# One sum and one reciprocal of a head's softmax sums in place of two

## The chip, the core and the metric

The kernel runs on one core of a Trainium2 chip. The metric is the device time in microseconds; the median of three runs of the kernel before is 1118.94 us (1118.8 to 1119.47).

The engines are named as in the profile: PE multiplies matrices (PEld are its weight loads), DVE is the vector engine, ACT computes the exponentials and many copies, POOL is GpSimd, SP issues the DMAs. Each engine works through its own queue strictly in the order in which the program was written; semaphores hold an instruction back until what it reads has been written.

## What is computed

Attention with a block-causal mask for 64 heads (batch 8, 8 heads, 576 positions, 64 channels), then a mixer: a low-rank product over the positions and a feed-forward pair of layers over the channels.

```python
scores = scale * np.matmul(q, k.transpose(0, 1, 3, 2))
...
scores = np.where(mask, scores, -1000000000.0)
scores = scores - np.max(scores, axis=-1, keepdims=True)
attn = np.exp(scores)
attn = attn / (np.sum(attn, axis=-1, keepdims=True) + 1e-09)
return np.matmul(attn, v).astype(np.float32)
...
h = xt @ U @ V
u = x + h.transpose(0, 2, 1)
ch = np.maximum(u @ w_ch1, 0.0) @ w_ch2
return (u + ch).astype(np.float32)
```

## The kernel before

**Tiles of a head.** The 576 query rows of a head are cut into five tiles: tile 0 has 64 rows and 64 keys, tiles 1 to 4 have 128 rows and 192, 320, 448 and 576 keys, since the mask lets a row see only the keys up to its block.

**The way of a head.** `softmax` is called three times per head: for tiles 4, 1 and 0 together, for tile 3, and for tile 2. Each call puts the score products on PE (L1233 for the first 14 heads, L1237 and L1238 for the rest), the row maxima on DVE (L1251, into mx), and the exponentials on ACT (L1262, into the tiles p). An exponential also writes the sum of its row into column 0 of ss; column 1 holds the constant 1e-9. `normalise` then adds the two columns (L1278, DVE), takes the reciprocal (L1279, DVE, into rv), and scales each tile p by it on POOL (L1289). Then `transpose` turns the tiles on PE (L1326), copies the result out of its bank on ACT (L1300, ph) and takes the remainder on DVE (L1343, pl), and `apply_v` multiplies with v (L1367 for the first 14 heads, L1383 for the rest). After two heads `mix` does the low-rank product for them (L1409 to L1456).

Before the change `normalise` is called twice per head: once for tiles 4 and 3, as soon as their exponentials are through, and once for tiles 2, 1 and 0. The tiles p, the sums ss, the maxima mx and the reciprocals rv have two buffers each, one for even and one for odd heads.

**The filler.** The feed-forward layers are in two parts. The first (hidden channels 0 to 767, `ffn_chunk`, products on L663 and L688) is given to the planner with a low priority on PE and runs between attention's products once its weights are ready. The second (`block_products`, L912) starts when attention is over and fills the rest of the time.

**What sets the order.** No loop of the source is the order on the engines. Every piece of work is handed to a planner with `add(engine, ns, prio, fn, reads, writes)`: an assumed duration, a priority and the buffers that it reads and writes. `issue` then plays this plan through in assumed time: an engine that is free takes, of the work whose inputs are ready and whose buffers are free, that with the lowest priority number, and writes its instructions into its queue. The order so found is fixed in the program. Each assumed duration is first shifted by up to 2% in a pseudo-random way that depends on the piece's number and on the constant `VARIANT` (L61), so that another `VARIANT`, or one piece more or less, gives other orders everywhere:

```python
ns *= 1 + 0.04 * ((n * 40503 + 7919 * VARIANT) % 65536 / 65536 - 0.5)
```

[...]

Of the kernel before, what the change touches and what calls it, by code (L numbers as in the profile page):

```python
# [57 lines left out]
TAIL = {"PE": 165, "DVE": 78, "ACT": 105, "POOL": 20, "SP": 0}  # L58
INTO = {"PE": 355, "DVE": 60, "ACT": 60, "POOL": 200, "SP": 60}
NEAR, DL, PORT = 130, 3000, 200  # L60
VARIANT = 96  # L61
START = {"DVE": 5750, "ACT": 2750, "POOL": 3300, "SP": 700}
COL = 0.4555
LA, MP = 900.0, 500.0
# [83 lines left out]
class Plan:  # L148
# [8 lines left out]
    def add(self, engine, ns, prio, fn, reads=(), writes=(), hold=(), after=0, port=False):  # L157

        n = len(self.tasks)
        ns *= 1 + 0.04 * ((n * 40503 + 7919 * VARIANT) % 65536 / 65536 - 0.5)  # L160
        deps = set()
        for b in reads:
            deps.update(b.writers)
            b.readers.append(n)
        for b in hold:
            deps.update(b.readers, b.writers)
        for b in writes:
            deps.update(b.readers, b.writers)
            b.writers, b.readers = [n], []
        deps.discard(n)  # L170
        slots = {b for b in (*reads, *writes) if b.pool is not None}
        for b in slots:
            b.users += 1
        self.tasks.append((engine, ns, prio, fn, deps, after, slots, port or engine == "POOL"))
# [105 lines left out]
def attention_then_mixer(  # L280
# [19 lines left out]
    add = plan.add  # L300
# [94 lines left out]
    inverse = [[Buf(iv_t[:, n, x : x + 1]) for x in range(1 + B)] for n in range(3)]  # L395
# [87 lines left out]
    def first_w1(w, bufs, prio, o, gate=()):  # L483
        at = lambda k: (slice(None), k, slice(o * C1, (o + 1) * C1))
        weights_of(
            {"gate": gate, "out": bufs["w1"][o]}, lambda k: w()["w1h"][at(k)], lambda k: w()["w1l"][at(k)],
            [w1[k * P : (k + 1) * P, 2 * o * C1 : 2 * (o + 1) * C1] for k in range(KC)], scales[o], prio, None, C1,
        )
# [34 lines left out]
    def first_w2(w, bufs, prio, o, gate=()):  # L523
        at = lambda k: (slice(None), o * FH + k, slice(None))
        weights_of(
            {"gate": gate, "out": bufs["w2"][o * FH : (o + 1) * FH]}, lambda k: w()["w2h"][at(k)], lambda k: w()["w2l"][at(k)],
            [w2[(o * FH + k) * P : (o * FH + k + 1) * P, :] for k in range(FH)], scales[2 + o], prio, agree if o else None,
        )
        multiply(inverse[o][B], scales[o], scales[2 + o], 2.0 ** -9, prio(FH - 1))
# [655 lines left out]
    def split_v(h, pr):  # L1185
        s = h % 2
        raw, vs = vr_r[h // 2 % 2], vs_r[s]
        mine = raw[:, 5 * s : 5 * s + 5, :]
        if s == 0:
            add(  # L1190
                "SP", 910, pr,
                lambda: nc.sync.dma_start(out=raw[:, 0:10, :], in_=v[h // 2].rearrange("p s j d -> p (s j) d")),
                writes=[raw], after=DL,
            )
        if h < FP:
            return
        hi, lo = vs[:, :, 0:64], vs[:, :, 64:P]
        add(
            "ACT", _act(320, True), pr, lambda: nc.scalar.copy(hi, mine),
            [raw], [vs],  # L1200
        )
        add("POOL", 845, pr, lambda: nc.gpsimd.tensor_sub(lo, mine, f32(hi)), [raw, vs], [vs])
# [69 lines left out]
    def normalise(h, tiles, pr):  # L1272
        ss, rv = ss_r[h % 2], rv_r[h % 2]
        cs = slice(min(tiles), max(tiles) + 1)

        def inverse():

            nc.vector.tensor_reduce(out=rv[:, cs], in_=ss[:, cs, :], op=ALU.add, axis=AX.X)  # L1278
            nc.vector.reciprocal(rv[:, cs], rv[:, cs])  # L1279

        add("DVE", 274, pr, inverse, [ss.parts[i] for i in tiles], [rv.parts[i] for i in tiles])
        for i in tiles:
            rows, w = P if i else 64, P * i + 64
            pt = pt_r[i][h % PB[i]]
            x = pt[:rows, :w]
            to = pt_r[1][h % PB[1]]
            add(
                "POOL", 255 + 0.85 * w, pr,
                lambda x=x, rows=rows, i=i, to=to: nc.gpsimd.tensor_scalar(  # L1289
                    out=x if i else to[:rows, P : P + 64], in0=x, scalar1=rv[:rows, i : i + 1], scalar2=1.0, op0=ALU.mult,  # L1290
                    op1=ALU.mult,
                ),
                [rv.parts[i], pt], [pt if i else to],
            )
# [188 lines left out]
    for h in range(NH):  # L1483
        pr = 1000.0 * h
        if h + 1 < NH:
            split_qk(h + 1, max(pr - LA, 1.0))
        for g, tiles in ((1, (4, 3)), (0, (2, 1, 0))):
            for x in ((4, 1, 0), (3,)) if g else ((2,),):
                softmax(h, x, pr + 10)
            normalise(h, tiles, pr + 10)  # L1490
        for g in (1, 0):
            for part in range(2):
                transpose(h, g, part, pr + 20 + 10 * (1 - g))
            apply_v(h, g, pr + 30)
        if h + 1 < NH:
            split_v(h + 1, pr + 1000)
        if h % 2 == 1:
            mix(h // 2, pr + 40)
        if h == min(WH, NH - 1):
            gate = Buf()  # L1500
            gate.writers = [len(plan.tasks) - 1]
            first_w2(lambda: wa, wab, lambda n: WPB + WP1 * n, 0, [gate])
            first_w1(lambda: wa, wab, lambda n: WP2 + WP3 * n, 1, [gate])
            first_w2(lambda: wa, wab, lambda n: WP4 + WP3 * n, 1, [gate])
# [48 lines left out]
```

## Time and profile before

| | us |
|---|---|
| median of 3 runs | 1118.94 |
| the profiled execution, its time | 1121.03 |
| its span (first to last instruction) | 1119.2 |
| PE, matmuls busy in the span | 1098.7 |
| DVE busy | 986.2 |
| ACT busy | 814.8 |
| POOL busy | 497.5 |

The granted clock of PE is 1.0 in the profiled execution. Matmul ends are modelled, and matmuls overlap, so that a start-to-start distance says more than one matmul's duration. The chain of work that ended last is mostly PE, with ACT's exponentials and DVE behind it:

```profile
PE 63%; ACT 15%; DVE 13%; DMA 4%; issue 3%; POOL 2%; SPq 0%; ACTq 0%; POOLq 0%; DVEq 0%
```

Of the lines that the change touches, POOL's scaling is the costliest group of the whole page by one line (its columns: busy us, mean ns of one, then POOL's idle time just before them and what ended it):

```profile
L1289 POOL TENSOR_SCALAR p<-p,rv 128x448 f32<-128x448 f32 (+4 forms) x320 | 170.3, 543 | 110.3 <-DVE rv L1279 25.5
```

### The profile page before, as it was taken

How to read it: one execution, taken by the hardware profiler on the slowest of the kernel's cores; microseconds unless marked ns; L12 is line 12 of the kernel's file. 1: busy time of each engine (PE TensorE's matmuls, PEld its weight loads, DVE VectorE, ACT ScalarE, POOL GpSimd, SP SyncE). 2: the span in 40 equal slices, each digit the busy share in tenths (PEclk: the TensorE clock that was granted, in tenths of full speed). 3: DMA queues.
4: the chain of work that ended last, by engine and by line, in shares of the span. 5: the costliest groups of instructions: out<-in, count | busy, mean ns of one | idle time of the engine just before them, and what ended most of it. 6: DMA issues, size and time to landing. Idle time of an engine off the chain costs nothing.

```text
span 1119.2 us, 25191 instructions
## 1 busy us (share of the span) xinstructions
PE 1098.7 (98%) x8846; PEld 915.3 (82%) x8846; DVE 986.2 (88%) x2241; ACT 814.8 (73%) x1994; POOL 497.5 (44%) x688
## 2 busy tenths in 40 slices
PE   9999999999999999999999999999999999999998
PEld 7877788888888888888888877777777777777776
DVE  5898898999898998998989767599989999998998
ACT  7887999998989999998988955255555445454543
POOL 5434468887878868778777774100000000000000
PEclk9999999999999999999999999999999999999999
DMA  4544567455454546464452152113223040403111
GB/s 127 160 121 123 155 179 190 132 158 153 118 158 137 151 129 167 115 198 131 137 142 80 40 151 66 44 34 95 75 54 103 27 117 12 128 19 110 34 52 44
DMA packets 76718, 122.11 MB, mean 109 GB/s; under 512 B 9008, under 2 KB 53040, under 8 KB 76592
## 3 DMA queue, kind: packets, MB, share of 16 engines
q1 hardware_dynamic: 76592, 120.51, 37.9%
q8 instruction: 70, 1.15, 0.4%
q14 instruction: 56, 0.46, 0.1%
HBM read 76.23 MB, written 29.49 MB: 94 GB/s over the span
## 4 chain that ended last, share of the span: by engine, by line
PE 63%; ACT 15%; DVE 13%; DMA 4%; issue 3%; POOL 2%; SPq 0%; ACTq 0%; POOLq 0%; DVEq 0%
PE bb L912 37%; ACT p L1262 6%; PE bf L663 6%; PE bf L688 5%; PE ba L1326 4%; DVE pl L1343 3%; DVE mx L1251 3%; PE ba L1383 2%; PE ba L1367 2%; ACT ph L1300 2%; DMA raw<-in_qk_dram 2%; PE bw L1233 1%; ACT tmp L1389 1%; ACT q L1173 1%; POOL p L1289 1%
## 5 line engine op out<-in xcount | busy, mean ns | idle before, releaser
L1289 POOL TENSOR_SCALAR p<-p,rv 128x448 f32<-128x448 f32 (+4 forms) x320 | 170.3, 543 | 110.3 <-DVE rv L1279 25.5
L912 PE MATMUL bb<-ph,w2h 128*128 128x288 f16 x560 | 151.0, 286 | 0.0
L912 PE MATMUL bb<-ph,w2l 128*128 128x288 f16 x560 | 151.0, 286 | 0.0
L912 PE MATMUL bb<-ph,w1h 128*128 128x288 f16 x560 | 148.7, 286 | 0.0
L912 PE MATMUL bb<-ph,w1l 128*128 128x288 f16 x560 | 148.7, 286 | 0.0
L834 ACT CAST ph<-hb 128x576 f16<-128x576 f32 x144 | 84.3, 590 | 83.5 <-PE bb L912 77.8
L912 PEld LDWEIGHTS <-w1h 128*128 128x128 f16 x1120 | 109.6, 98 | 27.5
L912 PEld LDWEIGHTS <-w2h 128*128 128x128 f16 x1120 | 109.6, 98 | 27.5
L912 PE MATMUL bb<-pl,w2h 128*128 128x288 f16 x560 | 123.6, 286 | 0.0
L1343 DVE TENSOR_TENSOR pl<-ba,ph 128x512 fp32r<-128x512 f32 x200 | 106.5, 550 | 10.1 <-ACT ph L1300 7.5
L912 PE MATMUL bb<-pl,w1h 128*128 128x288 f16 x560 | 114.5, 286 | 0.0
L688 PE MATMUL bf<-hh,w2h 128*128 128x288 f16 x384 | 110.3, 287 | 0.1
L688 PE MATMUL bf<-hl,w2h 128*128 128x288 f16 x384 | 109.8, 286 | 0.0
L688 PE MATMUL bf<-hh,w2l 128*128 128x288 f16 x384 | 109.8, 286 | 0.0
L1326 PE MATMUL ba<-ident,p 128*128 128x128 f32 x704 | 106.8, 274 | 2.4 <-POOL p L1289 1.1
L1262 ACT ACTIVATE p<-bw,mx 128x576 f32<-128x576 f32 (+2 forms) x192 | 93.0, 490 | 10.3 <-DVE mx L1251 8.7
L1300 ACT CAST ph<-ba 128x512 fp32r<-128x512 f32 x200 | 94.0, 493 | 3.1 <-PE ba L1326 1.3
L836 DVE TENSOR_TENSOR pl<-hb,ph 128x576 f16<-128x576 f32 x144 | 91.3, 651 | 1.2 <-ACT ph L834 0.4
L688 PEld LDWEIGHTS <-w2h 128*128 128x128 f16 x768 | 75.3, 98 | 20.4 <-issue 1.7
L663 PEld LDWEIGHTS <-w1h 128*128 128x128 f16 x768 | 73.4, 98 | 21.0 <-issue 3.9
L1383 PE MATMUL ba<-ph,vs 128*128 128x256 f32 (+3 forms) x400 | 86.4, 271 | 0.6 <-ACT p L1262 0.5
L1326 PEld LDWEIGHTS ba<-ident,p 128*128 128x128 f32 x704 | 82.2, 141 | 5.3 <-POOL p L1289 2.2
(185 smaller groups left out, 3091.9 us busy)
## 6 DMA issues: line engine op xcount, KB each, us to landing
raw<-in_qk_dram SPq DMA_DIRECT2D x63, 288.0 KB, 3.9
o_d<-ot SPq DMA_DIRECT2D x72, 144.0 KB, 2.0
vr<-in_v_dram SPq DMA_DIRECT2D x32, 320.0 KB, 3.6
ur<-u_d SPq DMA_DIRECT2D x64, 144.0 KB, 2.7
wr<-o_d SPq DMA_DIRECT2D x32, 288.0 KB, 3.0
out_dram<-wr SPq DMA_DIRECT2D x31, 288.0 KB, 2.3
st<-in_w_dram SPq DMA_DIRECT2D x16, 512.0 KB, 4.0
u_d<-ut SPq DMA_DIRECT2D x28, 288.0 KB, 2.1
```

The source lines that it names most:

```text
L663: nc.tensor.matmul(ps[:, :T], w()[wn][:, k, fs], m[k].ap, start=(i == 0), stop=(i == len(ops) - 1))
L688: nc.tensor.matmul(ps[:, :T], w()[wn][:, f, ms], hs[f][x].ap, start=(i == 0), stop=(i == len(ops) - 1))
L834: add("ACT", _act(n * T, True), E, lambda: nc.scalar.copy(h.ap[:, :n, :], x[0]()), [x[1]], [h])
L836: "DVE", _dve(n * T), E, lambda: nc.vector.tensor_sub(l.ap[:, :n, :], x[0](), h.ap[:, :n, :]), [x[1], h], [l],
L912: nc.tensor.matmul(bank[:, i, :T], x()[:, w(k)], p.ap[:, k, :], start=first and n == 0, stop=last and n == len(ops) - 1)
L1251: lambda i=i, at=at: nc.vector.tensor_reduce(out=mx[: P if i else 64, i : i + 1], in_=view(i, at), op=ALU.max, axis=AX.XY if i == 4 else AX.X,
L1262: nc.scalar.activation(out.rearrange("p (j k) -> p j k", j=2) if i == 4 else out, view(i, at), AF.Exp, bias=mx[:rows, i : i + 1], accum_ou ...
L1289: lambda x=x, rows=rows, i=i, to=to: nc.gpsimd.tensor_scalar(out=x if i else to[:rows, P : P + 64], in0=x, scalar1=rv[:rows, i : i + 1], s ...
L1300: add("ACT", _act(n), pr, lambda: nc.scalar.copy(out(), inp()), reads, writes)
L1326: nc.tensor.transpose(out=to, in_=pt_r[i][h % PB[i]][:, j * P : (j + 1) * P], identity=perm.ap)
L1343: "DVE", _dve(m), pr, lambda: nc.vector.tensor_sub(pl[:, low], bank[:, :m], f32(ph[:, low])), [bank, bh], [bl]
L1383: nc.tensor.matmul(bank[0 : c.stop, a:n], vs[:, j, c], x[:, _at(g, j)], start=(i == 0), stop=(i == len(ops) - 1))
```

## The change

`normalise` is called once per head, after all three calls of `softmax`, for the five tiles together: one sum over five columns of ss and one reciprocal over five columns of rv, which depend on all five exponentials. The five scalings on POOL stay five instructions. The assumed duration of the pair is 300 ns in place of 274, and `VARIANT` is 191 in place of 96.

```diff
-VARIANT = 96
+VARIANT = 191
...
-        add("DVE", 274, pr, inverse, [ss.parts[i] for i in tiles], [rv.parts[i] for i in tiles])
+        add("DVE", 300, pr, inverse, [ss.parts[i] for i in tiles], [rv.parts[i] for i in tiles])
...
         for g, tiles in ((1, (4, 3)), (0, (2, 1, 0))):
             for x in ((4, 1, 0), (3,)) if g else ((2,),):
                 softmax(h, x, pr + 10)
-            normalise(h, tiles, pr + 10)
+        normalise(h, (4, 3, 2, 1, 0), pr + 10)
```

Since the planner is run anew, the queues of all engines differ from the first heads on. Three places follow.

DVE, in the middle of attention, the same head in both programs (rv are its reciprocals, ss its sums; mx are maxima of the next heads, pl and xl remainders, hl and ot the filler's). Before:

```order
L1456 TENSOR_REDUCE um_109<-ut_202 128x1
L1278 TENSOR_REDUCE rv_187<-ss_162 128x2
L1279 RECIPROCAL rv_187<-rv_187 128x2
L1415 TENSOR_TENSOR xl_198<-ba_96,xh_197 128x512
L1251 TENSOR_REDUCE mx_185<-ba_98 128x1
L1251 TENSOR_REDUCE mx_186<-bw 128x1 x2
L1251 TENSOR_REDUCE mx_186<-bw 64x1
L671 SCALAR_TENSOR_TENSOR hl<-bf_91,hh 128x288
L1415 TENSOR_TENSOR xh_197<-ba_97,xh_197 64x128
L1278 TENSOR_REDUCE rv_187<-ss_162 128x3
L1279 RECIPROCAL rv_187<-rv_187 128x3
```

Of the change, from the same L1456 on:

```order
L1456 TENSOR_REDUCE um_109<-ut_202 128x1
L361 SCALAR_TENSOR_TENSOR z_102<-st_100,z_102 128x320
L1278 TENSOR_REDUCE rv_187<-ss_162 128x5
L1279 RECIPROCAL rv_187<-rv_187 128x5
L1343 TENSOR_TENSOR pl_192<-ba_97,ph_190 128x512
L1343 TENSOR_TENSOR pl_192<-ba_98,ph_190 128x448
L1343 TENSOR_TENSOR pl_191<-ba_95,ph_189 128x64
```

In place of two pairs with seven rows between them there is one pair, with remainders of other heads behind it.

POOL, some nine heads later, again the same head in both (p_1_173 down to p_1_165 are the head's tiles 4 to 0; q and k are inputs of later heads, t belongs to `mix`). Before:

```order
L1289 TENSOR_SCALAR p_1_173<-p_1_173,rv_188 128x576
L1289 TENSOR_SCALAR p_1_171<-p_1_171,rv_188 128x448
L1179 TENSOR_TENSOR q_1_176<-raw_161,q_1_155 64x576
L1289 TENSOR_SCALAR p_1_169<-p_1_169,rv_188 128x320
L1430 TENSOR_TENSOR t_0_199<-tz_200,t_0_199 32x128
L1289 TENSOR_SCALAR p_1_167<-p_1_167,rv_188 128x192
L1180 TENSOR_TENSOR k_1_158<-raw_161,k_1_179 64x576
L1289 TENSOR_SCALAR p_1_167<-p_1_165,rv_188 64x64
```

Of the change:

```order
L1289 TENSOR_SCALAR p_1_173<-p_1_173,rv_188 128x576
L1289 TENSOR_SCALAR p_1_171<-p_1_171,rv_188 128x448
L1289 TENSOR_SCALAR p_1_169<-p_1_169,rv_188 128x320
L1289 TENSOR_SCALAR p_1_167<-p_1_167,rv_188 128x192
L1289 TENSOR_SCALAR p_1_167<-p_1_165,rv_188 64x64
L1179 TENSOR_TENSOR q_1_176<-raw_161,q_1_155 64x576
L1180 TENSOR_TENSOR k_1_158<-raw_161,k_1_179 64x576
L1179 TENSOR_TENSOR q_2_177<-raw_160,q_2_156 64x576
```

The five scalings stand as one block, and q and k behind it.

PE, at the start of the program, a piece of the difference (bw and bf are score banks, raw_161 and raw_160 the inputs of the second and the third head, ba_97 takes the first head's transposes):

```order
 L1233 MATMUL bw<-raw_161 128x192
 L1233 MATMUL bw<-raw_161 128x64
+L1233 MATMUL bf_90<-raw_160 128x448
 L1326 MATMUL ba_97<-ident,p_0_170 128x128
 L1326 MATMUL ba_97<-ident,p_0_172 128x128
```

A score product of the third head has moved ahead of the first transposes; before, it stood nine rows further on. Each line of the products is in PE's queue as often as before.

## The prediction

> **What bounds the kernel.** I read the page's first part, then the busy time by stretches.
>
> ```profile
> PE 1098.7 (98%) x8846; PEld 915.3 (82%) x8846; DVE 986.2 (88%) x2241; ACT 814.8 (73%) x1994; POOL 497.5 (44%) x688
> ...
> L663 PEld LDWEIGHTS <-w1h x768: 95/98/155, 97.1 to 702.3; 128*128 128x128 f16 x192
> ...
> L1278 DVE TENSOR_REDUCE rv<-ss x128: 135/151/160, 10.6 to 630.5; 128x2 f32<-128x4 f32 x64, 128x3 f32<-128x6 f32 x64
> ...
> 0.00:97.00 97.00, 90.67 (x536) 75.49 (x537) 77.41 (x244) 79.79 (x224) 45.87 (x87) 1.00 0.46 133
> 97.00:631.00 534.00, 524.68 (x4361) 453.43 (x4360) 482.28 (x1316) 489.95 (x1356) 400.77 (x561) 1.00 0.51 143
> 631.00:720.00 89.00, 87.53 (x725) 70.41 (x723) 57.19 (x95) 45.28 (x79) 50.89 (x41) 1.00 0.30 87
> 720.00:1119.00 399.00, 395.81 (x3232) 315.92 (x3229) 369.28 (x589) 199.73 (x338) 0.00 (x0) 1.00 0.22 63
> ...
> 750.00:1050.00 300.00, 300.00 (x2452) 239.63 (x2450) 279.29 (x443) 152.25 (x258) 0.00 (x0) 1.00 0.25 71
> ```
>
> The columns of a stretch are its length, then the busy time of PE, weight loads, DVE, ACT and POOL. I cut at two events: the first weight load of the filler (the feed-forward products of L663 and L688, queued between attention's) at 97.1 us, and the last softmax sum at 630.5 us. PE is busy in all four stretches. In the last 399 us, which the change doesn't reach, it stops only at the very end: from 750 to 1050 us it has no gap, 300.00 / 2452 = 0.122 us from one matmul to the next. Up to 720 us its idle time is 6.3 + 9.3 + 1.5 = 17.1 us, the difference of the first two columns. The number of matmuls on each line is the same in both programs, and the filler moves to wherever attention leaves room. So attention's own length is not the metric: **the time changes only by what PE waits in the first 720 us**. Removing all of that would give 1.5%; a shorter DVE by itself gives nothing. Hence the second view, PE's waits up to 650 us, by what ended them (us in total, times, longest).
>
> ```profile
> PE bw L1233 <- ACT p L1262: 2.1, 4, 1.4
> PE ba L1326 <- POOL p L1289: 1.7, 3, 1.1
> PE ba L1326 <- DVE xl L1415: 1.4, 3, 0.9
> ...
> PE ba L1326 <- DVE um L405: 1.0, 1, 1.0
> ...
> PE ba L1326 <- DVE ur L1444: 0.7, 2, 0.5
> ...
> PE bw L1237 <- ACT p L1262: 0.6, 2, 0.4
> PE ba L1326 <- DVE pl L1343: 0.6, 2, 0.4
> PE ba L1383 <- ACT p L1262: 0.5, 1, 0.5
> PE ba L1326 <- DVE xt L1391: 0.4, 1, 0.4
> ...
> PE bf L663 <- DVE hl L671: 0.3, 1, 0.3
> ...
> PE ba L419 <- DVE oneu L415: 0.3, 1, 0.3
> PE ba L1439 <- ACT p L1262: 0.2, 1, 0.2
> PE ba L1439 <- DVE xt L1391: 0.2, 1, 0.2
> ```
>
> DVE ended 1.4 + 1.0 + 0.7 + 0.6 + 0.4 + 0.3 + 0.3 + 0.2 = 4.9 us of them, the exponentials on ACT 2.1 + 0.6 + 0.5 + 0.2 = 3.4, POOL's scaling 1.7: 10.0 us in all. I count all three as reachable by DVE, since the exponentials take their maxima and POOL its reciprocals from it.
>
> **Removed: one sum and one reciprocal per head.** 64 heads had two pairs each.
>
> ```profile
> L1279 DVE RECIPROCAL rv<-rv 128x3 f32<-128x3 f32 x64 | 11.3, 176 | 2.4 <-DVE rv L1278 0.2
> L1279 DVE RECIPROCAL rv<-rv 128x2 f32<-128x2 f32 x64 | 10.8, 168 | 2.2
> L1278 DVE TENSOR_REDUCE rv<-ss 128x2 f32<-128x4 f32 x64 | 9.8, 153 | 9.7 <-ACT p L1262 7.9 <-POOL p L1289 1.1 <-POOL us L641 0.3
> L1278 DVE TENSOR_REDUCE rv<-ss 128x3 f32<-128x6 f32 x64 | 9.7, 151 | 3.5 <-ACT p L1262 2.4 <-POOL k L1180 0.8
> L1251 DVE TENSOR_REDUCE mx<-bw 64x1 f32<-64x64 f32 x64 | 13.2, 206 | 0.1
> ```
>
> A head pays 153 + 168 + 151 + 176 = 648 ns. A pair over five columns isn't in the trace. Its reciprocal: 168 ns at two columns and 176 at three, so about 192 at five (bounds 176 and 200). Its sum reads ten numbers: the rows for four and for six agree at about 152; the next one up, 64 numbers, has 206 (bounds 151 and 206). I take 152 + 192 = 344 ns, nearest to the small rows. **DVE saves 0.30 us a head, 19.5 us in all** (15.5 to 20.5 by the bounds). Most of it is hidden, since PE stands in filler meanwhile. What it is worth to PE I estimate from the load. Between 97 and 631 us DVE is busy 482.3 / 534 = 90.3%. Some 53 heads lie there; less 53 x 0.304 = 16.1 us it is 87.3%. Where an engine's queue grows as u / (1 - u), that is 9.3 against 6.9, a cut of 26%. **26% of 10.0 us is 2.6 us**, with bounds of 0 (all the waits come from fixed places of the order) and 10.0 (all of them go).
>
> **Moved: tiles 4 and 3 wait for tile 2.** DVE's queue in the section on the change shows what waits behind a sum that has to wait for the last exponential: the L1343 remainders, which PE's L1383 products need. POOL's queue there shows a head's five scalings as one block, and q and k of later heads behind all of it, which in the trace of before were threaded between:
>
> ```profile
> 413.11 1.41 POOL L1179 TENSOR_TENSOR q<-raw,q 64x576 fp32r<-64x576 f32 x1
> 414.51 0.52 POOL L1289 TENSOR_SCALAR p<-p,rv 128x320 f32<-128x320 f32 x1
> ```
>
> POOL's work per head is the same, so I cost that reordering at nothing; PE's cover is the filler again, and without it q would come after three more scalings, each no longer than the 0.52 us shown, so at most 1.6 us. How late tile 4 becomes, one head of the trace shows:
>
> ```profile
> 403.15 0.16 DVE L1278 TENSOR_REDUCE rv<-ss 128x2 f32<-128x4 f32 x1 [0.32 <-ACT p L1262]
> ...
> 403.61 1.36 POOL L1289 TENSOR_SCALAR p<-p,rv 128x576 f32<-128x576 f32 x2 [1.35 <-DVE rv L1279]
> ...
> 405.27 0.19 ACT L1262 ACTIVATION_READ_ACCUMULATOR p<-ba,mx 128x1 f32 x1
> ...
> 405.53 0.16 DVE L1278 TENSOR_REDUCE rv<-ss 128x3 f32<-128x6 f32 x1
> ```
>
> Tile 2's sum arrives at 405.46 and its pair starts at 405.53, 2.4 us after that of tiles 4 and 3; in one pair, tile 4 starts 2.4 us later. From 97 us on filler covers this, in runs of 12 matmuls like this one of the chain of work that ended last:
>
> ```profile
> 141.05 1.47 PE bf L663 x12
> ```
>
> Two such runs cover it, so I cost it at nothing there; without that cover it is 2.4 us a head. Before 97 us there is no filler, and the first head shows PE already waiting for POOL. PE's queue in the section on the change shows the third head's score product moved ahead of the first transposes. The trace of before at this place:
>
> ```profile
> 9.76 1.73 PE L1233 MATMUL bw<-raw 128*128 128x288 f32 x8 [0.21 <-ACT p L1262]
> ...
> 12.15 0.68 ACT L1169 ACTIVATE raw<-raw 64x576 f32<-64x576 f32 x1
> ...
> 12.62 0.66 PE L1326 MATMUL ba<-ident,p 128*128 128x128 f32 x4 [1.13 <-POOL p L1289]
> ...
> 13.77 0.92 PE L1233 MATMUL bf<-raw 128*128 128x448 f32 x2
> 14.52 0.27 PE L1326 MATMUL ba<-swap,p 128*128 128x128 f32 x1
> ```
>
> The moved product is the one at 13.77. Its input is scaled on ACT until 12.15 + 0.68 = 12.83 us (behind the same exponentials in both programs), after the transposes could have started at 12.62. PE is in order, so it stands longer, not shorter: about 0.3 us with the hand-over (0 if ACT runs earlier; 1.4 if the wait of 1.13 at the transposes comes on top). I take **+0.3 us**.
>
> **Sum**: -2.6 + 0.3 = -2.3 us. The profiled execution took 1121.0 us around its span of 1119.2, so 1118.7 in its terms; it lies 2.1 us above the median of the runs, 1118.94, which becomes **1116.6 us**.
>
> **Rivals.**
>
> (1) *PE's waits stay*. The new numbers of the planner reorder every queue, and 17 us of scattered waits of at most 1.4 us each come back at other places. For it: no row above names the sums themselves. Against it: POOL's scaling and the exponentials sit behind DVE. It gives 1118.9, give or take 2.
>
> (2) *Slower: the single pair comes too late before the filler begins.*
>
> ```profile
> L1278 DVE TENSOR_REDUCE rv<-ss x22: 140/151/159, 10.6 to 95.9; 128x2 f32<-128x4 f32 x11, 128x3 f32<-128x6 f32 x11
> ```
>
> Eleven heads have their sums in those 97 us (the row is that of this stretch). A bare head costs PE 2.4 us less a score product of the next head, 14.52 - 13.77 = 0.75 us, about 1.7 us. From two bare heads on the gain is gone (3.4 against 2.3); with four it is 6.8 - 2.3 = 4.5 us slower, 1123.4. For it: the wait of 1.13 us above. Against it: POOL's share of PE's waits is 1.7 us in all.
>
> (3) *DVE is the bound and its 19.5 us come off whole*: 1118.9 - 19.5 = 1099.4. For it: 90.3% between 97 and 631 us. Against it: PE is idle there for only 9.3 us, 17.1 up to 720, less than it needs. [...]
>
> **How the numbers follow.** The forecast, a gain of 1 to 6 us, has 0.47; rival 1 has 0.30, rival 2 0.20, rival 3 0.03. A measurement of this kernel can tell about 0.2%, 2.2 us, so "faster" begins below 1116.7. The forecast gives 0.34 to faster and 0.13 to no change; rival 1 gives 0.05, 0.22 and 0.03 (slower); rival 2 gives 0.01 to no change and 0.19 to slower; rival 3 goes to faster. Faster 0.42, same 0.36, slower 0.22. The range takes in most of the bound of the relief and rival 2 with four bare heads: 1111.5 to 1123.5. The forecast's own range is 1113 to 1118.
>
> **What would show it.** In the changed profile: 64 rows of L1278 and L1279 near 152 and 192 ns; DVE's busy time less by about 19 us; the last 399 us unchanged; PE's idle time up to 720 us at 13 to 16 us in place of 17.1, with fewer waits ended by DVE and the exponentials; at some 12 us a PE wait at L1233 in place of the one at L1326. It is wrong if PE's waits for POOL's scaling grow by more than 3 us before the filler, or if PE's idle time stays while the total moves.

## The result and the profile after

The change is slower by 0.6%: little, but clear of the noise. Its median is 1125.01 us (1123.79 to 1128.8, 4 runs) against 1119.2 us of the kernel before, run beside it (1118.8 to 1120.46, 4 runs); the ratio is 1.0057, 95% interval 1.0045 to 1.0069. The forecast of 1116.6 us had the wrong sign, and the time lies above the range.

Two of the page's parts, the busy time of each engine and the two groups of the pair (busy us, mean ns of one, idle time before them):

```profile
PE 1103.5 (98%) x8846; PEld 919.4 (82%) x8846; DVE 971.5 (86%) x2113; ACT 813.6 (72%) x1994; POOL 495.8 (44%) x688
...
L1279 DVE RECIPROCAL rv<-rv 128x5 f32<-128x5 f32 x64 | 12.2, 191 | 2.2
...
L1278 DVE TENSOR_REDUCE rv<-ss 128x5 f32<-128x10 f32 x64 | 10.0, 157 | 7.4 <-ACT p L1262 7.1
```

The stretches, cut as in the prediction (length, then busy time of PE, weight loads, DVE, ACT and POOL, then the granted clock):

```profile
0.00:97.00 97.00, 88.86 (x501) 73.23 (x502) 72.72 (x211) 77.47 (x217) 43.32 (x86) 0.95 0.43 130
97.00:631.00 534.00, 522.40 (x4321) 452.32 (x4320) 468.17 (x1207) 485.86 (x1348) 397.43 (x557) 1.00 0.51 142
631.00:720.00 89.00, 88.67 (x736) 71.75 (x735) 56.78 (x101) 48.95 (x92) 55.08 (x46) 1.00 0.27 81
...
750.00:1050.00 300.00, 300.00 (x2451) 239.62 (x2450) 279.66 (x445) 151.78 (x256) 0.00 (x0) 1.00 0.25 72
```

The pair is as short as foreseen, and the block that ends the program still runs without a gap: 2451 matmuls in 300 us, 2452 before. PE idles 8.1 us before 97 us (6.3 before the change) and 11.6 us from 97 to 631 us (9.3); up to 720 us it is 20.1 us in place of 17.1, where 13 to 16 were forecast. The clock is new: 0.95 in the first stretch, which was 1.00. So I read the first 250 us finer, in the busy time of PE (with its matmuls and its clock). The kernel before:

```profile
50.00:100.00 50.00, 46.62 (x285) 1.00 0.40 117
100.00:150.00 50.00, 47.16 (x349) 1.00 0.50 146
150.00:200.00 50.00, 49.10 (x406) 1.00 0.69 190
200.00:250.00 50.00, 49.14 (x418) 1.00 0.53 145
```

The change:

```profile
50.00:100.00 50.00, 45.36 (x255) 0.90 0.36 111
100.00:150.00 50.00, 49.12 (x351) 1.00 0.50 147
150.00:200.00 50.00, 46.04 (x381) 1.00 0.74 207
200.00:250.00 50.00, 48.11 (x402) 0.97 0.48 135
```

Of the matmuls, 30 fewer lie between 50 and 100 us, and 25 and 16 fewer in the two stretches from 150 to 250 us. PE's waits give the two largest single ones (us in total, times, longest), and the one that the prediction placed at 12 us:

```profile
PE ba L1326 <- DVE xt L1391: 2.8, 3, 2.3
...
PE ba L1326 <- DVE tz L1428: 1.7, 1, 1.7
...
PE bf L1233 <- ACT raw L1169: 1.4, 1, 1.4
```

The 1.7 stands at 70 us, and the timeline (start, duration, engine and line; in brackets the idle time before it and what ended it) shows whose it is:

```profile
70.20 0.55 ACT L377 ACTIVATE z<-st 128x384 f32<-128x384 f32 x1 [2.62 <-DMA st<-in_w_dram]
70.77 0.26 ACT L1427 COPY tb<-ba 32x128 f32<-32x128 f32 x1
...
71.06 0.28 DVE L1428 TENSOR_TENSOR tz<-ba,tb 32x128 f32<-32x128 f32 x1 [0.70 <-ACT tb L1427]
...
71.40 0.33 PE L1326 MATMUL ba<-swap,p 128*128 128x128 f32 x1 [1.70 <-DVE tz L1428]
```

ACT's queue stands 2.62 us for a piece of weights that is still on its way (L377, the magnitude of a weight piece), L1427 is behind it, DVE waits for that, and PE for DVE. The 2.3 at 182 us has a chain of the same kind behind it: ACT stands 2.92 us for another piece of weights, then come L1389 on ACT, L1391 on DVE, and PE. No softmax sum stands in either chain. Behind the first, the clock is at a half:

```profile
69.50:72.70 3.20, 1.40 (x11) 1.00 0.38 99
72.70:82.90 10.20, 8.91 (x23) 0.50 0.24 74
```

Three theories follow. **Late loads**: the two places where ACT stands on a weight transfer make the loss. **Order** (it contains the first): the planner, run anew with another constant and another pair, has drawn a worse order, and the merging itself costs nothing. **Merged sum**: one pair that waits for the last exponential costs in any order.

### The profile page after: what moved, and what is told of

It is laid out like the page before. It is cut to its first block, busy times and chain, and to the rows that moved or that the text cites. A ratio compares the mean times of both kernels' runs of the same rounds, so it can differ in the third digit from the quotient of the medians.

```text
span 1127.0 us, 25026 instructions
## 1 busy us (share of the span) xinstructions
PE 1103.5 (98%) x8846; PEld 919.4 (82%) x8846; DVE 971.5 (86%) x2113; ACT 813.6 (72%) x1994; POOL 495.8 (44%) x688
## 4 chain that ended last, share of the span: by engine, by line
PE 67%; ACT 14%; DVE 13%; issue 3%; DMA 2%; SPq 0%; POOL 0%; ACTq 0%; DVEq 0%; POOLq 0%
PE bb L912 37%; PE bf L663 7%; PE bf L688 6%; PE ba L1326 5%; ACT p L1262 5%; DVE mx L1251 3%; PE ba L1383 3%; PE ba L1367 3%; DVE pl L1343 2%; ACT ph L1300 2%; DMA st<-in_w_dram 1%; PE bw L1233 1%; DVE xt L1391 1%; ACT tmp L1389 1%; ACT q L1173 1%
## 5 line engine op out<-in xcount | busy, mean ns | idle before, releaser
L1289 POOL TENSOR_SCALAR p<-p,rv 128x576 f32<-128x576 f32 (+4 forms) x320 | 169.1, 542 | 75.6 <-DVE rv L1279 26.3
L1343 DVE TENSOR_TENSOR pl<-ba,ph 128x512 fp32r<-128x512 f32 x200 | 106.9, 551 | 14.8 <-ACT ph L1300 12.2
L688 PE MATMUL bf<-hh,w2h 128*128 128x288 f16 x384 | 110.4, 287 | 0.4 <-DVE ot L700 0.3
L688 PE MATMUL bf<-hl,w2h 128*128 128x288 f16 x384 | 109.8, 286 | 0.0
L688 PE MATMUL bf<-hh,w2l 128*128 128x288 f16 x384 | 109.8, 286 | 0.0
L1326 PE MATMUL ba<-ident,p 128*128 128x128 f32 x704 | 106.8, 274 | 0.9 <-DVE xt L1391 0.3
L1262 ACT ACTIVATE p<-bw,mx 64x64 f32<-64x64 f32 (+2 forms) x192 | 93.0, 491 | 7.8 <-DVE mx L1251 7.0
L688 PEld LDWEIGHTS <-w2h 128*128 128x128 f16 x768 | 75.3, 98 | 20.5 <-issue 1.5
L663 PEld LDWEIGHTS <-w1h 128*128 128x128 f16 x768 | 73.5, 98 | 21.0 <-issue 3.1
L1251 DVE TENSOR_REDUCE mx<-bw 128x1 f32<-128x576 f32 (+2 forms) x192 | 76.3, 432 | 11.7 <-PE bw L1233 9.5
L1326 PEld LDWEIGHTS ba<-ident,p 128*128 128x128 f32 x704 | 82.1, 141 | 4.7 <-issue 1.7
```

Source lines behind the costliest of these rows:

```text
L663: nc.tensor.matmul(ps[:, :T], w()[wn][:, k, fs], m[k].ap, start=(i == 0), stop=(i == len(ops) - 1))
L688: nc.tensor.matmul(ps[:, :T], w()[wn][:, f, ms], hs[f][x].ap, start=(i == 0), stop=(i == len(ops) - 1))
L1251: lambda i=i, at=at: nc.vector.tensor_reduce(out=mx[: P if i else 64, i : i + 1], in_=view(i, at), op=ALU.max, axis=AX.XY if i == 4 else AX.X,
L1262: nc.scalar.activation(out.rearrange("p (j k) -> p j k", j=2) if i == 4 else out, view(i, at), AF.Exp, bias=mx[:rows, i : i + 1], accum_ou ...
L1289: lambda x=x, rows=rows, i=i, to=to: nc.gpsimd.tensor_scalar(out=x if i else to[:rows, P : P + 64], in0=x, scalar1=rv[:rows, i : i + 1], s ...
L1326: nc.tensor.transpose(out=to, in_=pt_r[i][h % PB[i]][:, j * P : (j + 1) * P], identity=perm.ap)
```

## The experiments

Ratios are to the kernel before, run beside it, with 95% intervals.

### The constant and the pair, apart

`split_v191` is the kernel before with the constant of the change, `merged_v96` the change with the constant of before.

```diff
-VARIANT = 96
+VARIANT = 191
```

> The kernel before (two pairs per head) with the change's constant 191 alone, so with another order of all queues. Merged-sum theory: no slower than before, 1117 to 1121, since the two pairs are kept. Late-loads or spread-of-orders theory: anything between 1117 and 1127, by how many L377 rows stand too early in this order; where ACT waits for a weight transfer for more than 2 us in total, slower than 1121.

> The change (one pair per head) with the constant 96 of before. Merged-sum theory: slow again, 1123 to 1127. Late-loads or spread-of-orders theory: it need not be; 1116 to 1125, and its time goes with ACT's waits for weight transfers and not with one pair or two.

| | constant 96 | constant 191 |
|---|---|---|
| two pairs | 1118.28 us (before) | 1121.4 us, 1.0027 [1.0017, 1.0036] |
| one pair | 1134.97 us, 1.0147 [1.0134, 1.0160] | 1125.01 us (the change) |

Of the change's loss, 3.1 us come with the constant alone and 3.6 us with the pair under that constant. (The 1125.01 us were measured beside other runs of the kernel before, which took 1119.2; by the ratios the two parts are 0.27% and 0.30%, 3.0 and 3.4 us.) Under the other constant the pair costs 16.7 us, and 1134.97 us lies above what either theory expected. The two edits don't add up, which the order theory explains; that both columns are slower with one pair speaks for the merged sum. Two columns can't settle that.

### What DVE's relief is worth

The kernel before in its own order, without the second pair of a head; the reciprocals of tiles 2, 1 and 0 are set to 1 once, so these tiles stay unnormalised.

```diff
+    for r in rv_r: nc.vector.memset(r.ap, 1.0)
...
         def inverse():
+            if 4 not in tiles: return
```

> The kernel before in its own order, without the sum and reciprocal of tiles 2, 1 and 0 (64 pairs less on DVE; these tiles are scaled by 1, so they stay unnormalised). It measures DVE's relief by itself, with no row of any other queue moved. The prediction's term: 26% of 10.0 us, so 2.6 us faster, about 1116.5. Rival, PE's waits stay where the order put them: within 1 us of before.

Measured 1117.9 us (12 runs), 0.9996 [0.9987, 1.0004]. 64 pairs less on DVE, nothing moved, and no wait added: 0.4 us, at most 1.5 by the interval. The time doesn't follow DVE's load. (In its profile PE idles 13.9 us up to 720 us, less than the 17.1 of before. But that profiled run, 1116.75 us, is the fastest of its twelve, and the profiled run of before, 1121.03 us, is slower than nearly all runs of that kernel: two single profiles can't show a gain that the medians don't have.)

### The weight pieces on ACT

The change's order on every queue, but the two L377 rows that stood on a transfer go behind the three ACT rows that followed them.

```diff
-VARIANT = 191
+VARIANT = 191; LATE = {13: 3, 23: 3}
...
-                x = tasks[n][3]()
+                x = self.call(e, tasks[n][3])
```

> The changed kernel with two rows of ACT's queue moved: the first step on a weight block (L377), which stood on ACT waiting for its transfer at 70 us (2.62 us) and at 181 us (2.92 us), goes behind the three ACT rows that followed it. All other queues are the same row for row. Late-loads theory (the loss is ACT standing on a transfer in front of attention's copies, PE behind it, and the half clock that followed): PE's two stalls of 1.70 and 2.25 us and the 0.95 us after the first go, and with them the half-clock stretches near 73 and 202 us; about 1119 to 1120.5 us against before's 1119. Merged-sum theory (tiles 4 and 3 wait too long for their reciprocal): no more than 1 us of change from the changed kernel, 1123 to 1126. Spread-of-orders theory (many small differences): 1122 to 1124.

Measured 1123.72 us (6 runs, 1122.07 to 1127.86), 1.0053 [1.0036, 1.0070]: the change's 1.0057 within its interval. The stall of 2.3 us at 182 us is gone. L1427, now ahead of L377 in ACT's queue, starts at 69.65 us where it started at 70.77, but at 71 us the next input and the next copy take the stall's place:

```profile
71.21 0.69 ACT L1169 ACTIVATE raw<-raw 64x576 f32<-64x576 f32 x1 [0.69 <-DMA raw<-in_qk_dram]
...
73.65 0.33 PE L1326 MATMUL ba<-swap,p 128*128 128x128 f32 x1 [1.79 <-ACT spare L1300]
```

So it is shown that these two rows in their places aren't what the loss hangs on; its two runs at a granted clock of 1.0 took 1122.07 and 1123.01 us, still 4 us above before. It isn't shown that transfers don't matter at all, since another one (raw) stands in the new chain. How long ACT stands on a piece of weights also varies from run to run: 2.62 and 2.92 us in the profile of the change, 1.6 us at most in that of `no_wait` below, whose queues are in the same order.

### The merged sum without its wait

The change's order on every queue, but the pair works on columns 4 and 3 alone and so doesn't wait for tile 2; tiles 2, 1 and 0 stay unnormalised.

```diff
-        cs = slice(min(tiles), max(tiles) + 1)
+        cs = slice(3, 5)
```

> The order of the change on every queue, but the one pair of a head works on columns 4 and 3 alone, so it doesn't wait for the exponential of tile 2; the factors of tiles 2, 1 and 0 are set to 1 once, so these tiles stay unnormalised. Theory A (the wait of the merged sum for the last exponential is what costs): three to five us faster than the change, 1119 to 1122. Theory B (the order of the queues around it costs, not that wait): within 1.2 us of the change, 1122.5 to 1126, with the same two stalls at 70 and 181 us and some half-clock time behind them.

Measured 1125.16 us (6 runs, 1121.93 to 1126.59), 1.0056 [1.0041, 1.0071], the same as the change. In the order that the planner found for it, the single pair's wait costs nothing that can be measured: taking it away gains nothing. The pair keeps its late place in DVE's queue here, so what that place costs is not part of this test. (The profiled run had a full clock and no stall at 181 us; that part of the order theory's expectation was wrong.)

### The merged sum in the order of before

The plan of before is kept. The first pair is dropped, the five-column pair stands where the second was, and only the rows that need its result move behind it, 53 of PE's 13873. The lines stand 4 or 5 further down in this file. The core of the edit:

```diff
+    def emit(self, tc, behind, n):
+        self.waiting = sorted([*self.waiting, n], key=lambda m: (m == n, 0)); go = True
+        while go:
+            go = next((m for m in self.waiting if self.can(m)), None)
...
-        cs = slice(min(tiles), max(tiles) + 1)
+        cs = slice(0, 5); n = len(plan.tasks); one = pairs.pop(h, None); pairs[h] = n if one is None else None
+        if one is not None: plan.first[n] = one; plan.second[one] = n
```

> The order of before is kept as it stands: the pair of tiles 4 and 3 is dropped, the pair of five columns stands where the pair of tiles 2, 1 and 0 stood, and only the rows that need its result move behind it (53 of PE's 13873 rows, some 130 of DVE's). All of the computation is done. Theory A (a single, later pair costs by itself, in any order): three or more us slower than before, 1121 to 1124, with new idle time of PE in front of the transposes of p (L1326 or L1331 of this file, whose lines stand a few further down) that is waiting for DVE or POOL. Theory B (the loss is that of the newly planned order, the merging by itself costs and gains next to nothing): within 2 us of before, 1116 to 1120, no half-clock stretch, DVE about 15 us less busy.

Measured 1182.56 us (5 runs), 1.0577 [1.0564, 1.0591]. Both theories missed by far: the order theory expected no loss, the merged sum 3 to 6 us. The waits of POOL, then of PE:

```profile
POOL p L1294 <- DVE rv L1284: 53.8, 26, 7.8
...
PE ba L1331 <- POOL p L1294: 40.4, 29, 2.6
```

In the kernel before, POOL's scaling (L1289 there) waits for the pair as follows:

```profile
POOL p L1289 <- DVE rv L1279: 25.5, 15, 4.1
POOL p L1289 <- DVE rv L1278: 15.8, 6, 4.8
```

So POOL's waits for the pair grow from 41.3 to 53.8 us, and PE's transposes wait for POOL 40.4 us where they waited 1.7 (prediction, second view). That is the term that the prediction set to nothing "there": the cover by filler exists only if the order is planned for the later pair. These 38.7 us are the larger part of the 64. Most of the rest can lie with the granted clock, 0.981 in the profiled run: (1 - 0.981) x 1181.7 us is about 22 us (an estimate from these two figures, and an upper one, since PE would have been idle for some of that time anyway). In the change's own order only this is left of it, and on the weight loads alone (8.5 us before the change):

```profile
PEld ba L1326 <- POOL p L1289: 2.8, 9, 0.5
```

The planner has taken these waits out, and the question became what it paid for that.

### Six more constants, with two pairs and with one

The kernel before (`split`) and the change (`merged`), each with the constants 1 to 6; within a pair of kernels no edit differs but the pair (with its assumed duration, 274 or 300 ns). With one pair the planner has 64 pieces fewer, so that its order is another draw even under the same constant: a single difference says little, their mean says more. For `merged_v1`:

```diff
-VARIANT = 191
+VARIANT = 1
```

> Two pairs per head, constant 1: one more order of the kernel before. Of 1 to 4, each constant is run with two pairs and with one. Spread-of-orders theory: this lies 1 to 10 us above before's 1118.3, and over the four constants one pair is as often faster as slower than two. Merged-sum theory: two pairs are faster at nearly every constant, by 3 us or more on average.

> One pair per head, constant 1. Spread-of-orders theory: within 5 us of split_v1, on either side. Merged-sum theory: 3 us or more above split_v1. Late-loads theory: slower than split_v1 only if ACT waits longer for weight transfers here.

> Two pairs per head, constant 2; as for split_v1: 1119 to 1129 us.

> One pair per head, constant 2. Spread-of-orders theory: within 5 us of split_v2, on either side. Merged-sum theory: 3 us or more above it.

> Two pairs per head, constant 3; as for split_v1: 1119 to 1129 us.

> One pair per head, constant 3. Spread-of-orders theory: within 5 us of split_v3, on either side. Merged-sum theory: 3 us or more above it.

> Two pairs per head, the constant of the tie-break 4. Both theories: 1118 to 1138 us, as the other orders of two pairs have come out; it is the other half of the comparison with one pair under the same constant.

> One pair per head, the same constant 4. Merged-sum theory: slower than the two pairs of this constant by 3 us or more (mean of the five before: 7). Order theory: the difference has either sign and a size of up to 17 us, with no lean.

> Two pairs per head, the constant 5: 1118 to 1138 us by both theories, the other half of the comparison under this constant.

> One pair per head, the constant 5. Merged-sum theory: slower than the two pairs of this constant by 3 us or more. Order theory: either sign, up to 17 us.

> Two pairs per head, the constant 6: 1118 to 1138 us by both theories, the other half of the comparison under this constant.

> One pair per head, the constant 6. Merged-sum theory: slower than the two pairs of this constant by 3 us or more (mean of seven differences: 8.2, standard error 3.0). Order theory: either sign, up to 17 us.

(The five differences before constant 4 have a mean of 6.4, not the 7 that is written there. With two pairs, constants 1, 2 and 3 came out 3 to 9 us above the 1119 to 1129 us expected.) In the table, "left" counts the matmuls of L663 and L688 after the last softmax sum, and "busy" is PE's busy time from 650 to 720 us, both from the stretches of each profile. The ratios are those of the medians to the kernel before.

| constant | two pairs, us (ratio) | left | busy | one pair, us (ratio) | left | busy | one - two, us |
|---|---|---|---|---|---|---|---|
| 96 | 1118.28 | 528 | 68.57 | 1134.97 (1.0147 [1.0134, 1.0160]) | 474 | 64.09 | +16.7 |
| 191 | 1121.40 (1.0027 [1.0017, 1.0036]) | 513 | 68.58 | 1125.01 (1.0057 [1.0045, 1.0069]) | 537 | 69.67 | +3.6 |
| 1 | 1132.51 (1.0119 [1.0090, 1.0148]) | 540 | 66.10 | 1144.28 (1.0224 [1.0195, 1.0254]) | 474 | 62.96 | +11.8 |
| 2 | 1137.79 (1.0166 [1.0131, 1.0202]) | 457 | 56.62 | 1131.81 (1.0113 [1.0079, 1.0147]) | 420 | 57.50 | -6.0 |
| 3 | 1134.94 (1.0142 [1.0113, 1.0172]) | 480 | 59.91 | 1140.75 (1.0194 [1.0159, 1.0229]) | 460 | 60.15 | +5.8 |
| 4 | 1123.27 (1.0040 [1.0024, 1.0056]) | 546 | 68.07 | 1134.15 (1.0137 [1.0108, 1.0167]) | 480 | 58.71 | +10.9 |
| 5 | 1126.00 (1.0066 [1.0043, 1.0089]) | 500 | 63.58 | 1140.82 (1.0197 [1.0167, 1.0226]) | 474 | 58.54 | +14.8 |
| 6 | 1121.25 (1.0033 [1.0022, 1.0044]) | 534 | 67.92 | 1143.38 (1.0219 [1.0185, 1.0254]) | 415 | 55.34 | +22.1 |
| mean | 1126.9 | 512 | 64.9 | 1136.9 | 467 | 60.9 | +10.0 |

Two things can be read from it. The order alone spreads the kernels with two pairs over 20 us, 1118.3 to 1137.8. And one pair is slower in 7 of 8 constants, by 10.0 us on average with a standard error of 3.1 (from the spread of the eight differences; 3.5 if the two groups of eight are taken as unpaired). So the merging does cost, in the orders that this planner finds; the order theory in its pure form has fallen. The kernel before and the change are each the fastest of their eight, and how 96 and 191 were chosen isn't on record; the six other constants alone give 9.9 us, so the mean doesn't rest on that choice.

Where these 10 us lie, the matmuls of PE in each stage tell (means over the eight profiles of each kind):

| stage, us | two pairs | one pair | fewer |
|---|---|---|---|
| 0 to 97 | 531.1 | 518.4 | 12.8 |
| 97 to 250 | 1178.3 | 1158.9 | 19.4 |
| 250 to 630 | 3169.8 | 3156.6 | 13.1 |
| 630 to 740 | 856.3 | 821.1 | 35.1 |

The 80 that are missing at 740 us are 9.8 us at the gap-free 0.122 us each, as much as the spans differ. Somewhat less than half of them are lost about the end of attention, and 40% before 250 us. The granted clock of the profiled runs goes the same way: it is 0.998 on average with two pairs and 0.9925 with one. On spans of 1126 and 1135 us that is 2.3 and 8.5 us of clock not granted. So up to 6 of the 10 us may be lost as time at a lower clock, and not in the stalls themselves; this is an estimate from these two figures, and an upper one.

What happens about the end of attention, constant 6 shows best. The rows are PE's L663, then its L688, from the last softmax sum on, with two pairs:

```profile
630.50:740.00 109.50, 32.93 (x246) 1.00 0.23 71
...
630.50:740.00 109.50, 36.70 (x288) 1.00 0.23 71
```

With one pair, from its own last sum on:

```profile
653.00:740.00 87.00, 24.94 (x199) 0.90 0.26 79
...
653.00:740.00 87.00, 27.45 (x216) 0.90 0.26 79
```

Attention ends 22 us later, and of the filler 415 matmuls are left to stand beside its last heads and the way into the second feed-forward part, in place of 534. All of PE from 650 to 720 us, with two pairs:

```profile
650.00:720.00 70.00, 67.92 (x544) 1.00 0.30 92
```

With one pair:

```profile
650.00:720.00 70.00, 55.34 (x443) 0.88 0.25 79
```

PE's longest waits between 640 and 710 us with one pair; with two pairs, the longest of that stretch is 0.5 us:

```profile
PE bb L912 <- ACT ph L841: 7.8, 1, 7.8
PE ba L1439 <- POOL t L1430: 3.6, 1, 3.6
```

119 matmuls of filler are about 14.5 us at 0.122 us each (the gap-free spacing of the prediction), and PE stands 12.6 us longer there. The filler isn't all used up at that point, but what can run is: with one pair 127 of the 415 run up to 672.3 us, none from there to 690 us, and the other 288 after it. ACT makes an input of these (uh) from POOL's us, and POOL's us waits for the scale that comes from the last heads (iv):

```profile
682.65 0.98 POOL L641 TENSOR_SCALAR us<-ur,sc 128x288 f32<-128x288 f32 x2 [1.68 <-DVE iv L446]
683.19 0.91 ACT L646 CAST uh<-us 128x288 f16<-128x288 f32 x2 [7.04 <-POOL us L641]
```

Over all sixteen kernels, "left" and "busy" go together: the seven with 500 or more left are busy for 63.6 to 69.7 us of the 70 and the nine with 480 or fewer for 55.3 to 64.1. The reading is that with the later pairs filler goes into the holes of attention's middle and is missing at its end. That link is a correlation over sixteen orders; no run changed the amount of filler alone. It isn't the whole loss either: constant 1 with two pairs has 540 left and still takes 1132.51 us, and it is from 97 to 250 us that it falls behind, with 1136 matmuls where the mean is 1178. Under constant 6 itself, 71 of the 175 matmuls missing at 740 us are lost before 630 us.

The change under 191 is the exception among those with one pair: 537 left, 69.67 us busy. In its profile the loss lies from 50 to 250 us, as shown above.

## Why the prediction was wrong, step by step

- **PE is the bound, and the last 399 us don't change**: right. The 300 us are without a gap in both programs, and the rival with DVE as the bound is out a second time: 64 pairs less on DVE were worth 0.4 us.
- **The pair, 152 + 192 = 344 ns**: right, 157 + 191 = 348. The four old groups of the pair and the two new ones differ by 41.6 - 22.2 = 19.4 us. DVE's busy time fell by 14.7 only. The other groups didn't become longer: all groups added up fell by 22.0 us, from 1097.8 to 1075.8. But that sum is 112 us above the busy time of before, 986.2, since rows of DVE overlap in the trace and the busy time counts an overlap once; so a row's own length is more than DVE gains when it goes. (`no_second_pair` dropped rows of 21.0 us, and DVE's busy time fell by 10.4.) The saving of 19.5 us was mis-sized by that.
- **The relief, 26% of 10.0 us = 2.6 us**: too large. Measured alone: 0.4 us, -0.4 to 1.5. That is near the lower bound, which was said to hold if PE's waits come from fixed places of the order. The 26% rest on waits that grow as u / (1 - u) with DVE's load, which was the author's assumption; no run shows such a growth.
- **Moved: tile 4 starts 2.4 us later, covered by filler, "so I cost it at nothing there"**: this is the step that failed, and with it the premise that "the filler moves to wherever attention leaves room. So attention's own length is not the metric". Without a new plan the later tiles cost 64 us. With a new plan they cost 10.0 us on average over eight constants and 3.6 under that of the change. Filler is a stock: what covers a hole in the middle isn't there at the end, which is where somewhat less than half of the average loss lies. Under 191 itself that stock was not short; there the loss shows from 50 to 250 us, and `no_wait` shows that it is not the pair's wait as such. That leaves the order around it, without a row to name.
- **+0.3 us at the start**: right in place and size. The wait at L1233 came, 1.4 us, and the one of 1.13 us at L1326 went, which is 0.3 more. But it is the only price that the sum sets on a wholly new order, and the constant alone made that 3.1 us. The same wait of 1.4 us or more stands in all eight orders with one pair; with two pairs it is 0.3 us or none.
- **Rival 1, "PE's waits stay ... 1118.9, give or take 2"**: the right kind of cost, priced far too small, and not the whole of it. Eight orders with two pairs span 20 us where 4 were allowed. The constant alone (96 to 191) was 3.1 us, more than the whole forecast gain.
- **Rival 2, slower because of bare heads before the filler**: right in sign and roughly in stage, wrong in mechanism. PE did lose matmuls before 97 us, 501 where it had 536, but for the most part around the stall behind a weight transfer in ACT's queue. PE's waits for POOL's scaling, which were to grow, went from 1.7 us to none that the view lists, and taking the pair's wait away changed nothing.
- **Not in the prediction at all: the clock.** The four runs of the change go with the granted clock: 1123.79 us at 1.0, 1124.27 and 1125.76 at 0.998, 1128.8 at 0.994. Its profiled run is the slowest of these, so some 5 of its 7.8 us above the span of before go with the clock, and the median's loss is less than that profile suggests. The runs of `late_loads` and `no_wait`, which have its order (but for two rows of ACT), do the same: 1121.93 to 1123.01 us at 1.0, 1127.86 at 0.994. At a full clock the order still loses some 4 us to before.

What stays open: how the 3.6 us under 191 come about in single rows, since moving the two rows behind the stalls of the profile didn't take them away; what is lost before 250 us with one pair in general; and whether a planner that held filler back for the end would make the merging free. No complete version with one pair beats the kernel before, and no other constant with two pairs does.

## What to carry to other kernels

Filler that hides a delay is a stock, so a delay "covered by filler" is only free if filler that can run is left over when the delayed work ends; count what is left there before a cost is set to nothing. Where a planner draws the order of all queues, first measure how far the time spreads over its tie-breaks with nothing else changed: a forecast of 2 us is worth little where that spread is 20, and an edit is then compared over several draws, in pairs. DVE's load of 88% said little here on what its relief gives (0.4 us for 64 pairs), since another engine, PE, was busy for 98% of the span; leaving the work out in the old order measures it directly.

## What the chip showed that was not expected

The clock fell from 1.00 to 0.50 after short waits. The two rows at 69.5 and 72.7 us above show it: PE was busy for 1.40 of 3.20 us, in which no single wait was over 1.70 us, and then ran at 0.50 for 10.2 us. It happened again with 1.82 us busy of 3.40:

```profile
199.00:202.40 3.40, 1.82 (x20) 1.00 0.72 200
202.40:205.80 3.40, 3.40 (x17) 0.50 0.29 95
```

The longest waits there were 1.1 and 0.5 us. The length of one wait doesn't decide it: in `late_loads` the wait of 1.79 us that ended at 73.65 us left the clock at 1.00, as its row from 50 to 100 us shows:

```profile
50.00:100.00 50.00, 44.58 (x273) 1.00 0.42 125
```

At the handover of the slower orders the gaps are long: with constant 6 and one pair PE is busy for 5.34 us from 670 to 690 us, one of its waits is the 7.8 us shown above, and the clock there is 0.63.

```profile
670.00:690.00 20.00, 5.34 (x36) 0.63 0.56 179
```

So a stall can have a second price behind it, for PE that has work again: in the profile of the change, 10.2 us and 3.4 us at a clock of 0.50.
